# Splitting the tables' operands once on 128 rows, and a first DFT step on four row tiles of 32

## The chip, the cores and the metric

The kernel runs on one core of a Trainium2 chip. Its time is the device time of one execution in microseconds (us). A timed run and the profiled execution are different executions; the profile's times are counted from the start of the profiled span.

The core's engines work side by side, each through its own instructions in order: PE multiplies matrices (PEld is its loading of weights), DVE, ACT and POOL work on vectors, SP issues most DMA transfers here. ACT and POOL can issue transfers too. Results of PE land in PSUM and are copied ("evacuated") to SBUF by ACT or DVE.

## What is computed

Two independent parts, whose outputs stand side by side:

```python
def _A_ref(x, wqkv, wo):            # x: (1, 2048, 576), 32 heads of 18, window W = 256
    qkv = (x @ wqkv).reshape(B, S, 3, H, Dh).transpose(2, 0, 3, 1, 4)
    scores = einsum("bhqd,bhkd->bhqk", q, k) * Dh ** -0.5
    mask = (q_pos - k_pos >= 0) & (q_pos - k_pos < W)
    p = softmax(where(mask, scores, -1e9))
    return (p @ v).transpose(0, 2, 1, 3).reshape(B, S, D) @ wo

def _B_ref(u, A_re, A_im, B_re, B_im, C_re, C_im, log_dt, Dskip):   # D = 576, N = 128, L = 2048
    dt = exp(log_dt)[:, None]
    P = exp((dt * A)[:, :, None] * arange(L))            # complex
    K = einsum("dn,dnl,dn->dl", C, P, dt * B).real       # 2048 taps for each channel
    y = irfft(rfft(pad(u)) * rfft(pad(K)))[:L]           # causal convolution over L
    return y + u * Dskip

out = concatenate([_A_ref(...), _B_ref(...)], axis=-1)
```

Part A is attention over a sliding window; part B makes a kernel of 2048 taps for each of 576 channels from exponentials and convolves u with it.

## The kernel before

The program has four stages.

**Opening** (`front`, lines 208 to 300, an order written out by hand). It loads the projection's weights `wqkv` in four pieces into the tile `K`, x (two pieces `raw` for the first 512 columns, and the rest as four pieces `flat`, which share two buffers), and the parameters of part B. `amax` finds the largest absolute value of each piece on DVE; POOL reduces over the partitions (`pow2_max`), and from that a power of two scales weights and x. `split_w` and `split_x` split each into an f16 value and an f16 remainder: the first on ACT, the remainder on DVE.

In the same order the operands of the tables are made: `al` from A_re times dt, `ps` from A_im times dt over 2 pi. Both are bf16 tiles of 96 rows with three levels of the same 32 channels: rows 64 to 95 hold the rounded value, rows 0 to 31 the rounded remainder of it, rows 32 to 63 the remainder of that, so that one matmul over 96 rows adds up the levels. The host gives the inputs three times (96 x 18 x 128), and the subtractions run on 64 and then 32 of these rows: `al`'s on DVE (lines 255, 263, 271), `ps`'s on POOL (lines 265, 267, 279), the copies on ACT (256, 264, 266, 272, 278, 280).

**Joint stage** (lines 1006 and 1007). Three generators are merged in proportion to their lengths: `proj` (14 matmuls for each group of 128 output rows and 512 columns of x; line 171; results to DRAM as `qd` and `vd`), `tables` (36 chunks of 16 channels: exponentials on ACT, sines and cosines on ACT, products on POOL at line 411 and on DVE at 431 to 434, and then the taps, 64 small f32 matmuls at line 449), and `s1_u`, the first DFT step of u. The tables' first pieces, `exps_ab` and `exps_q` (12 matmuls and 12 exponentials), are part of this stage. PE's instructions keep the order that the program's scheduler gave them; the opening and the start of the attention stage keep the order of the code.

**First DFT step** (`s1`, lines 486 to 495). A step takes 4 of 64 values of l, 576 columns of f32. The 128 rows are four groups of 32 (four groups of channels, each with 32 points). Weight `w1` is 128 x 128 with the 32 x 32 cosine matrix four times on the diagonal, and another one with the sines. A step is two parts (cosine, sine) of two matmuls of 288 columns each, every one into its own PSUM buffer of the pool `pps` (three buffers, shared with the projection). `evac` copies each to SBUF, three of four on ACT and one on DVE, and one transfer a part, 288 KB, takes the 128 rows to DRAM: `gx` for u (16 steps in the joint stage), `gk` for the taps (16 steps after it, of which ten are merged with `gmax(0)`, the row maxima of the first attention unit: line 668 on PE, 675 on DVE).

**Attention and convolution** (line 1031). `load` (line 516) fetches for each of 16 pairs of frequencies the pieces `tx` of `gx` and `tk` of `gk`, 576 KB each in one transfer; the other DFT steps are interleaved with the attention.

Transfers issued by SP and ACT share a ring of semaphores: a transfer waits until the one that used the same semaphore before it has landed.

## Time and profile before

| | |
|---|---|
| median of 3 runs | 1023.63 us (1023.08 to 1027.1) |
| profiled execution | 1029.98 us |
| its span | 1028.3 us |
| mean granted PE clock | 0.968 |
| busy: PE, PE weight loads, DVE, ACT, POOL | 838.4, 449.0, 697.9, 568.5, 601.5 us |
| moved by DMA | 150.56 MB, 146 GB/s over the span |

The span lies 1.7 us inside the profiled execution's own time, which is 6.3 us above the median.

A row of a timeline has start, length, engine, line, operation, output <- input, shape, and in brackets the idle time of the engine before it with what ended it. "x8" counts instructions: an f32 matmul appears as two. Lengths of matmuls include the time until the result is out, so that neighbours overlap and a busy PE can stand for less work than its busy time. A row of a group has the summed busy time, the mean of one in ns, and the idle time of the engine ahead of them. A row of the stretches has the busy time and the count of instructions of each engine, the granted PE clock, the share of time in which the DMA engines were busy, and the rate.

### The profile page before, as it was taken

Reading aid. Unit: us, or ns where it says so; the run is one execution under the profiler, and the core shown is the slowest. Engines: PE = TensorE matmul, PEld = TensorE weight load, DVE = VectorE, ACT = ScalarE, POOL = GpSimd, SP = SyncE. Lnnn points to the kernel's source line nnn. Section 1 sums busy time; section 2 is a strip of 40 time slices with the busy share of each in tenths; the row PEclk is TensorE's granted clock in tenths of the full one; section 3 lists DMA queues with packets and bytes.
Section 4 is the critical chain, followed back from the end, with each engine's and each line's share of the span. In section 5 each row is a group of like instructions: output and inputs, shape, how many; then the busy total and the mean of one; then the engine's idle time right before and its main releaser. Section 6 shows DMA issues by size and latency. Waiting matters only on the chain.

```text
span 1028.3 us, 26833 instructions
## 1 busy us (share of the span) xinstructions
PE 838.4 (82%) x10364; PEld 449.0 (44%) x10364; DVE 697.9 (68%) x1799; ACT 568.5 (55%) x893; POOL 601.5 (58%) x717
## 2 busy tenths in 40 slices
PE   0079979999996989687888887778888999988687
PEld 0034644565564557454333333333333444444245
DVE  5957594676667565545677788778777766777454
ACT  0546675776765765234565555555655655644470
POOL 0424784786666666300567666767686766766670
PEclk9999999999998999989999899999999999999899
DMA  9744544545452433757444556446444464678863
GB/s 308 230 108 108 122 117 96 120 99 132 104 123 61 106 83 75 201 173 215 114 124 124 175 153 198 129 114 186 134 140 145 131 187 113 161 196 224 224 179 126
DMA packets 144711, 150.56 MB, mean 146 GB/s; under 512 B 36408, under 2 KB 121144, under 8 KB 143624
## 3 DMA queue, kind: packets, MB, share of 16 engines
q1 hardware_dynamic: 137896, 133.51, 47.1%
q0 software_dynamic: 6128, 14.60, 5.1%
q8 instruction: 81, 1.33, 0.5%
q10 hardware_dynamic: 560, 0.74, 0.2%
q14 instruction: 46, 0.38, 0.1%
HBM read 87.42 MB, written 61.01 MB: 144 GB/s over the span
## 4 chain that ended last, share of the span: by engine, by line
PE 25%; DVE 12%; issue 6%; DMA 6%; ACT 3%; POOL 2%; SPq 1%; DVEq 0%; POOLq 0%; ACTq 0%
PE r L668 5%; PE po L732 5%; PE r L938 4%; PE r L532 3%; PE r L540 3%; PE ST L709 3%; DVE jk L675 2%; PE pp L493 2%; DVE qb L659 2%; ACT P L711 1%; DVE osb L791 1%; DMA tx<-gx 1%; DMA raw<-in_wo_dram 1%; POOL P L720 1%; DVE t L562 1%
## 5 line engine op out<-in xcount | busy, mean ns | idle before, releaser
L675 DVE CUSTOM_DVE_ANT_0 jk<-r,bias 128x288 f32<-128x288 f32 (+7 forms) x512 | 199.9, 433 | 91.1 <-PE r L668 89.0
L720 POOL TENSOR_SCALAR_AFFINE_SELECT P<-P 128x512 f32<-128x512 f32 x240 | 167.2, 726 | 154.4 <-ACT P L711 151.9
L711 ACT ACTIVATE P<-ST,esc 128x1024 f32<-128x1024 f32 (+1 forms) x192 | 202.4, 1059 | 91.3 <-PE ST L709 90.7
L411 POOL TENSOR_TENSOR m<-A,tr 128x1024 f32<-128x1024 f32 x72 | 143.9, 2022 | 76.6 <-PE kp L449 76.6
L668 PE MATMUL r<-K,qb 128*64 128x288 f16 (+7 forms) x1024 | 129.2, 297 | 43.8 <-DVE qb L659 11.9
L668 PEld LDWEIGHTS <-qb 128*64 128x64 f16 x1024 | 59.8, 109 | 126.8 <-issue 68.3
L732 PE MATMUL po<-P,V 128*32 128x256 f32 (+2 forms) x1408 | 101.8, 404 | 15.7 <-ACT osb L740 6.0
L569 POOL TENSOR_TENSOR Y<-t,t 64x288 f32<-64x288 f32 x64 | 54.4, 850 | 74.7 <-DVE t L564 72.8
L493 PE MATMUL pp<-ut,w 128*128 128x288 f32 x128 | 41.5, 446 | 65.8 <-DMA ut<-in_u_dram 52.4
L449 PE MATMUL kp<-Q,m 128*32 128x64 f32 x4608 | 82.8, 225 | 9.2 <-DVE Q L432 5.2
L449 PEld LDWEIGHTS kp<-Q,m 128*32 128x32 f32 x4608 | 71.5, 113 | 34.9 <-issue 23.8
L709 PE MATMUL ST<-Q,K 64*128 64x384 f16 (+2 forms) x704 | 73.3, 282 | 0.0
L732 PEld LDWEIGHTS po<-P,V 128*32 128x32 f32 x1408 | 36.6, 111 | 50.7 <-issue 32.4
L493 PEld LDWEIGHTS pp<-ut,w 128*128 128x128 f32 x128 | 23.3, 199 | 79.8 <-issue 53.4
L136 ACT ACTIVATE g<-pp 128x288 f32<-128x288 f32 x96 | 37.4, 413 | 37.3 <-PE pp L493 27.8
L389 POOL TENSOR_TENSOR tr<-tr,mab 128x768 f32<-128x768 f32 x18 | 33.2, 1845 | 39.8 <-ACT tr L358 39.8
L570 POOL TENSOR_TENSOR Y<-t,t 64x288 f32<-64x288 f32 x64 | 53.6, 838 | 3.7
L352 DVE TENSOR_TENSOR k<-x,k 128x512 f32<-128x512 f32 (+1 forms) x54 | 33.9, 639 | 28.9 <-ACT k L351 28.7
L353 DVE TENSOR_SCALAR ab<-k 128x512 int32<-128x512 int32 (+1 forms) x54 | 53.0, 993 | 0.4
L171 PE MATMUL pp<-xh,wh 128*128 128x512 f16 x180 | 48.9, 392 | 4.1 <-DVE qst L318 2.7
L171 PEld LDWEIGHTS <-wh 128*128 128x128 f16 x324 | 31.6, 99 | 45.2 <-issue 11.7
L318 DVE SCALAR_TENSOR_TENSOR qst<-pp,qst 128x512 f16<-128x512 f32 x36 | 24.6, 685 | 36.0 <-ACT qst L317 21.3
(172 smaller groups left out, 1757.5 us busy)
## 6 DMA issues: line engine op xcount, KB each, us to landing
gx<-g SPq DMA_DIRECT2D x32, 288.0 KB
qd<-qst SPq DMA_DIRECT2D x72, 128.0 KB
gk<-g SPq DMA_DIRECT2D x32, 288.0 KB
tx<-gx SPq DMA_DIRECT2D x16, 576.0 KB
tk<-gk SPq DMA_DIRECT2D x16, 576.0 KB
h<-ho SPq DMA_DIRECT2D x16, 576.0 KB
Q<-qd SPq DMA_DIRECT2D x32, 216.0 KB
raw<-in_x_dram SPq DMA_DIRECT2D x8, 640.0 KB
```

The source lines that it names most:

```text
L171: self.nc.tensor.matmul(ps, u, v, start=(i == 0), stop=(i == len(ops) - 1))
L411: self.nc.gpsimd.tensor_tensor(m, A[:, ch, a0:a0 + 8].unsqueeze(3).to_broadcast(sh), tr[:, ch, part, 0:8].unsqueeze(2).to_broadcast(sh), o ...
L449: nc.tensor.matmul(kp[32 * st:32 * st + 32, c % 2 * JJ2 + j, :], m[:, ch, a0:a0 + 32], Q[:, ch, term % 2, :], start=(term == 0), stop=(ter ...
L493: nc.tensor.matmul(ps, self.w1[:, part, :], src[:, o:o + k], start=True, stop=True)
L569: nc.gpsimd.tensor_tensor(Y[par][0:64], t1[sl, 0], t2[sl, 0], op=OP.subtract)
L570: nc.gpsimd.tensor_tensor(Y[par][64:128], t1[sl, 1], t2[sl, 1], op=OP.add)
L668: nc.tensor.matmul(ps[64 * b:64 * b + 64, :n], self.qb[:, b, t, :], d["K"][:, b, k0:k0 + n], start=True, stop=True, skip_group_check=True)
L675: nc.vector.tensor_tensor_reduce(out=jk[:, :n], in0=ps[:, :n], in1=self.bias[:, 288 - n:], scale=1.0, scalar=-3e38, op0=OP.add, op1=OP.max ...
L709: nc.tensor.matmul(ps[:, u, o:o + n], d["K"][h, jp, k0:k0 + 128], d["Q"][h, jp, q0:q0 + n], start=True, stop=True, skip_group_check=True)
L711: nc.scalar.activation(pt[:, 2 * jp:2 * jp + 2, lo:hi], ps[:, :, lo:hi], AF.Exp, scale=self.esc)
L720: nc.gpsimd.affine_select(v, v, pattern=[[0, 4], [sg, 128]], compare_op=OP.is_ge, fill=0.0, base=-1 if far else 0, channel_multiplier=-sg)
L732: nc.tensor.matmul(self.po[32 * j:32 * j + 32, t0 * 128:t1 * 128], V[:, kb * 76 + 19 * j:kb * 76 + 19 * j + 32], pt[:, j, o:o + (t1 - t0) ...
```

## The change

**Operands of the tables.** The host now lays A_re, A_im and log_dt out on 128 rows (`by_group`): four blocks of 32 rows with five groups of channels each (the last block has three), 128 x 5 x 128, once and not three times. On these tiles `level(i)` multiplies by dt (i = 0) or subtracts the last level, on DVE for both operands, and rounds to bf16 on ACT into one of six small tiles `part`. Four transfers for each level and operand spread the blocks to rows 32 i to 32 i + 31 of `al` (issued by ACT) and `ps` (issued by POOL): 24 transfers of 32 rows, SBUF to SBUF. POOL's tensor operations in the opening are gone. The loads of A_re and A_im are issued by ACT ahead of the constants.

**Order of the opening.** The tables' first twelve pieces (`exps_ab(0)`, `exps_ab(1)`, `exps_q(0)`) are called from `front`, between the splits of the weights. The four pieces of `flat` have a buffer each. The remainders of the weights' last two pieces (`split_w(2, 1)` and `(3, 1)`) are called from `proj`. The first merge ahead of the long one takes six parts of the projection and four of the tables, and none of `s1_u`; before, it took 7, 16 and 1. The long merge has 50, 308 and 16 parts instead of 49, 308 and 15.

**First DFT step.** `w1` is 128 x 64: in each block of 32 rows the cosines and then the sines. A half step is four matmuls of 32 rows (one block each) and 64 columns, at four row positions and, in turns, two column positions; two of them fill the two halves of one PSUM buffer. A step has eight matmuls instead of four, four evacuations as before, and four transfers of 64 rows (144 KB) instead of two of 128. For the taps the second half's two buffers come from a new PSUM pool `s1p`. `gx` and `gk` have a new layout (64, 4, 64, 144), and `load` fetches `tx` and `tk` in two transfers of 64 rows each.

```diff
-    w1 = np.zeros((128, 2, 128))
-    for s in range(4):
-        w1[s * 32:s * 32 + 32, 0, s * 32:s * 32 + 32] = np.cos(ph)
-        w1[s * 32:s * 32 + 32, 1, s * 32:s * 32 + 32] = np.sin(ph)
+    w1 = np.tile(np.concatenate([np.cos(ph), np.sin(ph)], axis=1), (4, 1))
...
+def by_group(v):
+
+    w = np.zeros((4, 5, GC, v.shape[1]), np.float32)
+    w.reshape(20, GC, -1)[:NQ] = v.reshape(NQ, GC, -1)
+    return np.ascontiguousarray(w.transpose(0, 2, 1, 3).reshape(128, -1))
...
         for c in range(4):
-            flat.append(tp.tile([128, 2304], F32, name="flat%d" % (c % 2))[:, :cols[c + 1] - cols[c]])
+            flat.append(tp.tile([128, cols[c + 1] - cols[c]], F32, name="flat%d" % c))
...
+        parts = [[tp.tile([128, 5, 128], BF, name="part%d%d" % (e, i)) for i in range(3)] for e in range(2)]
+        ops = [(nA["A_re"], dtn, al, nc.scalar), (nA["A_im"], dtp, ps, nc.gpsimd)]
+
+        def level(i):
+
+            for e, (z, d, T, eng) in enumerate(ops):
+                if i == 0:
+                    tt(z, z, wide(d), op=OP.mult)
+                else:
+                    tt(z, z, parts[e][i - 1], op=OP.subtract)
+                act(parts[e][i], z, AF.Copy)
+            for e, (z, d, T, eng) in enumerate(ops):
+                for r in range(4):
+                    n = min(5, NQ - 5 * r)
+                    eng.dma_start(T[32 * i:32 * i + 32, 5 * r:5 * r + n], parts[e][i][32 * r:32 * r + 32, :n])
+
+        self.mab, self.mg = {}, {}
+        exps = chain(self.exps_ab(0), self.exps_ab(1), self.exps_q(0))
         for c in range(4):
             self.amax(amx[:, c:c + 1], wf[:, c])
+            if c < 3:
+                level(c)
...
+        next(exps), next(exps)
         self.split_w(0, 0)
...
-    def s1(self, src, g, l0, nl, pool):
+    def s1(self, src, g, l0, nl, pool, psum):
+
         nc, n = self.nc, nl * 144
-        for part in range(2):
-            st = self.p[pool].tile([128, n], F32, name="g1")
-            k = n // 2 if n <= 576 else n // 3
-            for o in range(0, n, k):
-                ps = self.p["pps"].tile([128, 512], F32, name="pp")[:, :k]
-                nc.tensor.matmul(ps, self.w1[:, part, :], src[:, o:o + k], start=True, stop=True)
-                self.evac(st[:, o:o + k], ps)
-            nc.sync.dma_start(g[part, l0:l0 + nl].rearrange("l p j -> p l j"), st.rearrange("p (l j) -> p l j", j=144))
+        st = [self.p[pool].tile([128, n], F32, name="g%d" % e) for e in range(2)]
+        k = n // 2
+        for i in range(2):
+            ps = [self.p[psum[i]].tile([128, 512], F32, name="pp")[:, :k] for _ in range(2)]
+            for q in range(4):
+                r, h = slice(32 * q, 32 * q + 32), 64 * (q % 2)
+                nc.tensor.matmul(ps[q // 2][h:h + 64], self.w1[r], src[r, i * k:i * k + k], start=True, stop=True,
+                                 skip_group_check=True)
+            for e in range(2):
+                self.evac(st[e][:, i * k:i * k + k], ps[e])
+        for q in range(4):
+            h = 64 * (q % 2)
+            nc.sync.dma_start(g[l0:l0 + nl, q].rearrange("l p j -> p l j"),
+                              st[q // 2][h:h + 64].rearrange("p (l j) -> p l j", j=144))
...
-                nc.sync.dma_start(t[nm], g.rearrange("a l (s f) j -> (a l) s f j", s=4)[:, :, 2 * fp:2 * fp + 2, :])
+                for e in range(2):
+                    f0 = 32 * e + 2 * fp
+                    nc.sync.dma_start(t[nm][64 * e:64 * e + 64], g[:, :, f0:f0 + 2])
...
-                merge((part(proj, 7), 7), (part(tables, 16), 16), (part(s1u, 1), 1))
-                merge((proj, 49), (tables, 308), (s1u, 15))
-            self.pool(ek, "s1k", 4, side="right")
+                merge((part(proj, 6), 6), (part(tables, 4), 4))
+                merge((proj, 50), (tables, 308), (s1u, 16))
+            self.pool(ek, "s1k", 2, side="right")
+            self.pool(ek, "s1p", 2, PSUM, side="right")
```

The numbers of lines in what follows are those of the kernel before.

More of the change, by code (lines that the diff above doesn't have):

```diff
@@ L2 @@
 from contextlib import ExitStack
+from itertools import chain
 import ml_dtypes
@@ L1000, in build @@
                 proj, tables, s1u = self.proj(), self.tables(), self.s1_u()
+                for n in ("mab", "mg"):
+                    self.pool(e1, n, 4)
                 with ExitStack() as e2, self.tc.manual_schedule():
```

69 lines of the change are left out of this document (28 added, 41 removed).

## The prediction

> **What bounds the kernel now.** I read the profile by stages: the busy time per stretch first, then the timeline of the opening, the groups of the joint stage, and the chain of waits through the first DFT step of the kernel taps. The stretches (length; busy time of PE, PE weight loads, DVE, ACT, POOL, each with its count; granted PE clock; DMA share; GB/s):
>
> ```profile
> 25.00:52.00 27.00, 0.00 (x0) 0.00 (x0) 25.83 (x12) 14.04 (x7) 10.47 (x2) 1.00 0.72 228
> 52.00:60.00 8.00, 4.03 (x9) 2.35 (x10) 4.76 (x9) 5.58 (x6) 0.38 (x1) 1.00 0.20 44
> 60.00:92.00 32.00, 29.04 (x115) 12.12 (x114) 17.51 (x23) 17.34 (x27) 7.25 (x2) 0.95 0.46 112
> 92.00:420.00 328.00, 294.62 (x5731) 187.12 (x5730) 215.05 (x312) 213.39 (x383) 231.37 (x187) 0.98 0.44 104
> 420.00:437.00 17.00, 12.21 (x38) 7.45 (x38) 8.53 (x11) 4.83 (x12) 0.00 (x0) 0.90 0.90 257
> 437.00:467.00 30.00, 26.70 (x131) 16.91 (x132) 14.44 (x70) 10.99 (x27) 0.00 (x0) 0.89 0.58 169
> 475.00:1028.00 553.00, 465.33 (x4320) 218.62 (x4316) 395.30 (x1344) 294.89 (x420) 349.54 (x518) 0.97 0.55 158
> ```
>
> Four stages follow each other. In the opening (to 60 us) PE does almost nothing and DVE is full. From 60 to 420 PE is full and every other engine has room: this is the joint stage of projection, tables and u's first DFT step. From 420 to 475 runs the kernel's first DFT step, held by DMA until 437 and then by a loop through PE and DVE. The attention stage behind it is not rewritten, so I let it move as a whole.
>
> The opening in the timeline (start, length, engine and line):
>
> ```profile
> 18.30 2.40 DVE L161 TENSOR_REDUCE amx<-K 128x1 f32<-128x2160 f32 x1 [1.45 <-DMA K<-in_wqkv_dram]
> 22.12 2.55 DVE L255 TENSOR_TENSOR nA_re<-nA_re,dtn 96x2304 f32<-96x2304 f32 x1 [1.23 <-DMA nA_re<-in_n_A_re_dram]
> 25.23 2.87 DVE L161 TENSOR_REDUCE amx<-raw 128x1 f32<-128x1280 f32 x2
> 28.85 2.47 DVE L192 SCALAR_TENSOR_TENSOR wl<-K,wr,wh 128x2160 f16<-128x2160 f32 x1 [0.75 <-ACT wh L190]
> 31.23 6.39 DVE L263 TENSOR_TENSOR res<-nA_re,al 64x2304 f32<-64x2304 f32 x1
> 37.55 5.00 DVE L161 TENSOR_REDUCE amx<-flat 128x1 f32<-128x2304 f32 x2
> 40.11 0.35 SPq L231 DMA_DIRECT2D flat<-in_xf_dram  x1
> 42.57 6.31 DVE L271 TENSOR_TENSOR res<-res,al 32x2304 f32<-32x2304 f32 x1
> 48.91 2.61 DVE L161 TENSOR_REDUCE amx<-flat 128x1 f32<-128x1152 f32 x2
> 51.56 0.16 DVE L145 TENSOR_REDUCE xm<-amx 128x1 f32<-128x6 f32 x1
> 54.38 2.61 ACT L201 ACTIVATE xh<-raw,xr 128x1280 f16<-128x1280 f32 x2 [5.75 <-DVE xr L157]
> 60.29 0.15 PEld L171 LDWEIGHTS <-wh 128*128 128x128 f16 x1
> ```
>
> The projection cannot start before x's maximum is known (51.56) and x is split (54.38 on). DVE reaches that maximum late because two subtractions on whole tables, 6.39 and 6.31 us, stand ahead of it, and because the third piece of `flat` is issued only at 40.11, when DVE has read the first two.
>
> ```profile
> 65.71 1.24 PE L171 MATMUL pp<-xh,wh 128*128 128x512 f16 x5
> 68.73 1.24 PE L171 MATMUL pp<-xh,wh 128*128 128x512 f16 x5
> 70.89 1.03 PE L171 MATMUL pp<-xl,wh 128*128 128x512 f16 x4
> 74.57 2.02 PE L171 MATMUL pp<-xh,wh 128*128 128x512 f16 x5 [2.66 <-DVE qst L318]
> 90.39 1.82 POOL L389 TENSOR_TENSOR tr<-tr,mab 128x768 f32<-128x768 f32 x1 [24.12 <-ACT tr L358]
> 92.27 2.39 PE L493 MATMUL pp<-ut,w 128*128 128x288 f32 x8
> ```
>
> A row group of the projection is 14 matmuls. The first takes 5.4 us (60.29 to 65.71), the second 3.02 (to 68.73), and after the third (ended 71.92) PE waits until 74.57. The tables' twelve exponentials are interleaved only then, so POOL gets its first table at 90.39. The second, long merge begins on PE at 92.27 and lasts to the first matmul of the kernel's DFT near 419.8: 327.5 us.
>
> **The opening after the change.** On DVE two multiplications and four subtractions of 128x640 take the place of 96x2304. By the 2.55 us of the multiplication one costs 2.55 x 640/2304 = 0.71; by the 6.39 us of the subtraction 1.78. I take 0.71 for all, since the two long subtractions ran beside POOL's own tensor work, which is gone. Six are 4.3 us and lie between the four maxima of the weights, where DVE waits for loads (1.45 us ahead of the last). So the weight maxima still end near 20.7. At the dear price 8.5 us lie there, some 4 more than the gaps hide.
>
> The 24 spreading transfers are issued half by ACT and half by POOL. POOL's last four stand ahead of the reduction over partitions; a POOL issue costs 0.61 us by this group, 2.4 us for four:
>
> ```profile
> L798 POOL DMA_DIRECT2D od<-oh x52 | 31.6, 610 | 0.0
> L358 ACT ACTIVATE mg<-x 128x512 f32<-128x512 f32 x64 | 35.9, 599 | 4.9 <-PE x L341 4.3
> ```
>
> That puts the weights' scale near 25.3, where it was (DVE went on at 25.23). Then DVE runs raw maxima 2.87, flat maxima 5.00 + 2.61, and three `wl` of 2.47 (one is pulled ahead of x's maximum in the new order): 25.3 + 2.87 + 7.61 + 7.41 = 43.2 instead of 51.56. With four buffers no `flat` waits for DVE. ACT's twelve exponentials, at most 12 x 0.60 = 7.2 us, fit in, since ACT is busy 14.04 of 27.00 there. From the maximum to the split takes 54.38 - 51.56 = 2.82, the split 2.61: the projection starts near 50 with some reserve for late operands (60.29 before; bounds 47 and 56, the latter if ACT's issues are held behind loads).
>
> From there to the long merge the old order had six row groups, the exponentials and two idle stretches, 32.0 us. The new one has five row groups and no exponentials: one at 5.4 (slow at first, as it will be again) and four at 3.02, 17.5, plus about 1.5 for stalls on evacuation: 69 instead of 92.3, bounds 65 and 80 (the earliest and the latest start above, without stalls and with the old idle time beside it). **Opening: -23**, of which +3.0 comes back, since one row group more stands inside the long merge.
>
> **First DFT step of u.** Before: four matmuls of 128x128 a step; after: eight of 32 rows and 64 columns, each half the output. What concurrency looks like here:
>
> ```profile
> 545.41 1.19 PE L532 MATMUL r<-tk,w 128*64 128x288 f32 x8
> 547.38 0.39 PE L709 MATMUL ST<-Q,K 64*128 64x384 f16 x4
> 547.95 1.21 PE L540 MATMUL r<-Y,i 128*128 128x288 f32 x4 [0.18 <-DVE t L565]
> ```
>
> Eight instructions on two column tiles take 1.19, four on the whole array 1.21: two column tiles run side by side in f32. Row tiles are shown only in pairs of 64 rows and in f16 (four in 0.39 us). Row tiles of 32 in f32 are shown nowhere. The step's PE time was 2.14 (eight instructions, 0.267 each); all four side by side it is 1.07, pairs only 2.14, none 4.28. I take 1.25.
>
> But a step costs the joint stage more than its matmuls:
>
> ```profile
> L493 PE MATMUL pp<-ut,w 128*128 128x288 f32 x112 | 34.8, 430 | 13.4 <-ACT g L136 8.8 <-DVE qst L318 2.6 <-ACT vst L329 1.9
> 218.25 1.46 PE L493 MATMUL pp<-ut,w 128*128 128x288 f32 x4
> 220.39 1.54 PE L493 MATMUL pp<-ut,w 128*128 128x288 f32 x4 [0.67 <-ACT vst L329]
> ```
>
> Fourteen steps are 34.8 busy and 13.4 waiting for PSUM buffers, 3.44 each (the one at 218.25 took 3.6). Now a half step takes two of the three buffers at once, and the second half waits for the projection's tile and for the first evacuation. I take 2.8: fifteen steps at 3.44 were 51.6, sixteen (one more lies in the merge) at 2.8 are 44.8. **u: -7**; bounds +3 (still 3.44) and -20 (2.0, matmuls plus the evacuations' 0.4).
>
> The Trainium skill, TensorEngine Tiling (Array Packing), section PSUM Bottleneck, says that tiling speeds up the matmuls but not the emptying of PSUM. By its rule all four evacuations remain and the gain is smaller than the 0.9 us of PE time; the idle column above agrees.
>
> **First DFT step of the kernel.** One round of the loop with the row maxima:
>
> ```profile
> 454.24 2.14 PE pp L493 x8
> 456.38 0.39 PE r L668 x4
> 456.79 0.45 DVE jk L675
> 457.30 0.31 PE r L668 x2
> ```
>
> ```profile
> 454.96 1.43 ACT L136 ACTIVATE g<-pp 128x288 f32<-128x288 f32 x3 [1.94 <-PE pp L493]
> 437.01 0.71 ACT L136 ACTIVATE g<-pp 128x288 f32<-128x288 f32 x2 [5.04 <-DMA gk<-g]
> 480.00:484.00 4.00, 3.44 (x30) 1.43 (x28) 3.51 (x20) 1.80 (x2) 0.64 (x1) 0.87 0.99 319
> ```
>
> A round is 3.37 us (454.24 to 457.61), of which 2.14 is the step. At 1.25 it is 2.5; ACT's 1.43 and two extra PSUM buffers fit. Seven such rounds give 6.2, the two longer rounds before 444 some 2, the burst at the end 1. The first 17 us stay, because there the stores set the pace (5.04 us for a landing). A step stores 0.59 MB, in 2.5 us 236 GB/s, against 319 at a full DMA share; four issues like that at 40.11 (0.35) take 1.4. I take 2 off: **kernel: -7**, bounds 0 and -9.
>
> In the convolution each fetch becomes two, 32 issues more on SP, of 0.35 us like that at 40.11, 11 us spread over more than 350; no engine's wait is added, so 0 to +3 for a later landing, taken as 0.
>
> **Sum:** -23 + 3 - 7 - 7 = -34. The profiled execution took 1029.98 (span 1028.3), so it would be 996; the median of the runs is 1023.63, 6.3 lower, so 990.
>
> **The rivals.** (1) *Row tiles gain nothing.* Only two of the four tiles run at a time, because two share the columns, or because the first and second write one PSUM tile and the third and fourth the other: u stays 3.44 a step (+3), the kernel's round 3.37. -23 + 3 + 3 = -17: 1007. For it: no f32 row tile in the trace; against: the pairs at 547.38, though these write two PSUM banks. The Trainium skill, TensorEngine Tiling (Array Packing), Gotcha 1: PSUM Pressure, says that different row tiles cannot use one PSUM bank at the same time; by it this rival would hold, and no row here shows two row tiles in one bank.
>
> (2) *Operands late.* ACT's issues wait for loads ahead of them and hold the copies, exponentials and `wh` behind them on ACT; PE waits for all three levels. The opening gives 5 instead of 23: 1008. For it: the DMA share is still 0.72 after 25 us, when these transfers run; against: each is only 41 KB (32 rows of 640 bf16).
>
> (3) *Stores in halves are slow.* Every transfer of the DFT now spans 64 partitions. If one ran at half of 319 GB/s, 9.4 MB of stores take 59 us plus the loads among them, +8 instead of -7, and the attention's first fetch +7: -23 + 3 - 7 + 8 + 7 = -12: 1012. Against it: two are in flight together. The Trainium skill, DMA: Bandwidth & Descriptors, Rules for kernel authors, says that transfers to disjoint partition halves serialize and one of 128 partitions should be used; it speaks for this rival, and no row here compares the two.
>
> (4) *Slower: no overlap at all.* If the four f32 row tiles follow one another, a step is 4.28: u 16 x 5.58 - 51.6 = +38, the kernel's later eleven steps 11 x 2.14 = +24 and the first five +4. -23 + 3 + 38 + 28 = +46: 1070. With 27 steps that count (sixteen and eleven), -20 is used up at 2.14 + (20 - 3)/27 = 2.8 us a step; from there it decides. Against it: 545.41.
>
> **How the numbers follow.** Forecast 0.57; (1) 0.13, (2) 0.11, (3) 0.09, (4) 0.08; 0.02 for no change. The forecast's own range is 978 to 1000. Including (1), (2) and most of (3) the range is 975 to 1013; what is left out is (4) and the tails. Within 0.5% means 5 us, about what can be told from no change. Faster gets 0.85, same 0.05, slower 0.10.
>
> **What would show it.** The first `wh` load near 50 and POOL's first table near 63; the u group's busy plus idle near 2.8 us a step; rounds of 2.5 us; the kernel's DFT beginning near 392 and ending near 440; the attention stage still 553. Wrong if an eight-matmul burst takes over 2 us, if the first `wh` comes after 56, or if the attention stage grows by over 5.

## The result, and the profile after the change

| | kernel before | changed kernel |
|---|---|---|
| median on the same chip | 1024.83 us | 1029.84 us |
| ratio of the times | | 1.0063, 95% interval 1.0046 to 1.0080 |
| profiled execution, its span | 1029.98, 1028.3 us | 1032.46, 1030.7 us |
| mean granted PE clock | 0.968 | 0.948 |
| to the projection's first matmul | 60.8 us | 60.2 us |
| joint stage, to the first matmul on the taps | 359.0 us | 361.7 us |
| first DFT step of the taps, to the first score matmul | 53.1 us | 52.5 us |
| attention and convolution, to the end | 555.4 us | 556.3 us |

The change makes the kernel slower by 0.6%, about 5 us, where 34 us faster was forecast; the time lies above the range. No stage is shorter by more than 1 us. The stages are those of one profiled execution each. The one of the kernel before lies 5.2 us above its median and that of the changed kernel 2.6, so the stages show only 2.4 of the 5 us. The stretches of the changed kernel, at the same times as in the prediction (length; busy time of PE, weight loads, DVE, ACT, POOL; granted clock; DMA share; GB/s):

```profile
25.00:52.00 27.00, 7.11 (x15) 1.77 (x16) 13.94 (x13) 13.17 (x17) 2.34 (x5) 1.00 0.75 244
52.00:60.00 8.00, 0.00 (x0) 0.00 (x0) 5.98 (x9) 2.42 (x2) 0.35 (x1) 1.00 0.00 0
60.00:92.00 32.00, 29.55 (x189) 12.44 (x191) 24.69 (x36) 16.08 (x28) 15.36 (x13) 1.00 0.53 125
92.00:420.00 328.00, 294.80 (x5772) 173.78 (x5761) 205.44 (x300) 205.57 (x372) 215.07 (x171) 0.94 0.46 103
437.00:467.00 30.00, 20.70 (x204) 9.53 (x204) 15.25 (x73) 10.35 (x28) 0.00 (x0) 0.75 0.84 196
```

DVE, full from 25 to 52 before (25.83 us busy), is now busy for 13.94 of 27 us: its two long subtractions are gone, and yet the projection starts no earlier. From 92 to 420 PE is busy as long as before (294.80 against 294.62 us), but the granted clock has fallen from 0.98 to 0.94. From 437 to 467 PE has 6 us less to do, and the DMA engines are busy for 0.84 of the time instead of 0.58.

The changed kernel's opening, in its own line numbers (150 the maxima's last reduction, 151 POOL's reduction over partitions, 158 its first use, 176 the projection, 206 the split of x, 269 the spreading transfers):

```profile
25.10 0.16 DVE L150 TENSOR_REDUCE wm<-amx 128x1 f32<-128x4 f32 x1
26.70 1.96 POOL L269 DMA_DIRECT2D ps<-part  x4 [2.67 <-ACT part L265]
37.76 0.38 POOL L151 PARTITION_ALL_REDUCE wg<-wm  x1 [9.11 <-issue]
38.17 0.15 DVE L158 TENSOR_SCALAR wg<-wg 128x1 f32<-128x1 f32 x1 [12.92 <-POOL wg L151]
56.18 0.15 DVE L150 TENSOR_REDUCE xm<-amx 128x1 f32<-128x6 f32 x1
60.25 1.86 PE L176 MATMUL pp<-xh,wh 128*128 128x512 f16 x4 [9.22 <-ACT xh L206]
```

The weights' maximum is there at 25.10, when the forecast had its scale (25.3). But POOL first issues its last four spreads (1.96 us), and then does nothing that the profile names for 9.11 us ("issue": it waits for nothing that the profile shows) before it reduces. DVE stands idle for 12.92 us. Everything behind it takes what the prediction gave it: from the scale to x's maximum it is 56.18 - 38.17 = 18.0 us, forecast 43.2 - 25.3 = 17.9. The joint stage and the first DFT steps, by groups (busy, mean, idle time ahead and its causes), and two rounds of the taps' loop:

```profile
L509 PE MATMUL pp<-ut,w 32*64 32x288 f32 x256 | 30.7, 440 | 9.5 <-DVE qst L333 4.7 <-ACT g L141 4.1
L141 ACT ACTIVATE g<-pp 128x288 f32<-128x288 f32 x48 | 17.8, 409 | 34.7 <-DMA gk<-g 24.7 <-PE pp L509 9.9
452.69 1.20 PE L509 MATMUL pp<-K,w 32*64 32x288 f32 x16
455.16 1.20 PE L509 MATMUL pp<-K,w 32*64 32x288 f32 x16
460.35 1.20 PE L509 MATMUL pp<-K,w 32*64 32x288 f32 x16
463.56 1.20 PE L509 MATMUL pp<-K,w 32*64 32x288 f32 x16
```

A burst of eight matmuls takes 1.20 us (1.25 forecast, 2.14 before): four row tiles in f32 do run side by side. A step of u costs PE (30.7 + 9.5) / 16 = 2.5 us with its waits, less than the 2.8 of the forecast. In the loop of the taps the first round is 2.47 us, as forecast, the last one shown 3.21, and the evacuations wait 24.7 us for the stores of `g` (7.2 before).

So three questions are open: what holds the reduction, why less PE work in u does not shorten the joint stage, and what the stores cost.

### The profile page after: what moved, and what is told of

It is laid out like the page before. It is cut to its first block, busy times and chain, and to the rows that moved or that the text cites. A ratio compares the mean times of both kernels' runs of the same rounds, so it can differ in the third digit from the quotient of the medians.

```text
span 1030.7 us, 27519 instructions
## 1 busy us (share of the span) xinstructions
PE 833.3 (81%) x10620; PEld 423.5 (41%) x10620; DVE 688.7 (67%) x1802; ACT 556.8 (54%) x893; POOL 589.1 (57%) x726
## 4 chain that ended last, share of the span: by engine, by line
PE 43%; DVE 19%; issue 12%; DMA 11%; ACT 8%; SPq 4%; POOL 2%; DVEq 0%; ACTq 0%; POOLq 0%
PE pp L176 11%; PE r L691 5%; PE po L755 5%; PE r L961 4%; PE kp L466 4%; PE r L555 3%; PE ST L732 3%; PE r L563 3%; PE x L358 2%; DVE jk L698 2%; PE pp L509 2%; DMA gk<-g 2%; SPq L130 2%; ACT P L734 1%; DVE qb L682 1%
## 5 line engine op out<-in xcount | busy, mean ns | idle before, releaser
L691 PE MATMUL r<-K,qb 128*64 128x288 f16 (+7 forms) x1024 | 131.7, 304 | 45.3 <-DVE t L586 11.5
L466 PE MATMUL kp<-Q,m 128*32 128x64 f32 x4608 | 80.2, 222 | 8.0 <-issue 3.6
L176 PE MATMUL pp<-xh,wh 128*128 128x512 f16 x180 | 51.7, 408 | 16.5 <-ACT xh L206 10.7
L755 PEld LDWEIGHTS po<-P,V 128*32 128x32 f32 x1408 | 36.2, 110 | 50.1 <-issue 33.2
L141 ACT ACTIVATE g<-pp 128x288 f32<-128x288 f32 x96 | 35.7, 411 | 37.4 <-DMA gk<-g 24.7
L333 DVE SCALAR_TENSOR_TENSOR qst<-pp,qst 128x512 f16<-128x512 f32 x36 | 24.7, 686 | 45.8 <-ACT qst L332 42.0
L555 PE MATMUL r<-tx,w 128*64 128x288 f32 x256 | 42.4, 440 | 11.5 <-ACT X L582 5.4
L176 PE MATMUL pp<-xh,wl 128*128 128x512 f16 x180 | 51.5, 413 | 0.0
L370 DVE TENSOR_SCALAR ab<-k 128x512 int32<-128x512 int32 (+1 forms) x54 | 47.5, 892 | 0.3
```

Of the source, the lines that this page charges most:

```text
L176: self.nc.tensor.matmul(ps, u, v, start=(i == 0), stop=(i == len(ops) - 1))
L466: nc.tensor.matmul(kp[32 * st:32 * st + 32, c % 2 * JJ2 + j, :], m[:, ch, a0:a0 + 32], Q[:, ch, term % 2, :], start=(term == 0), stop=(ter ...
L555: nc.tensor.matmul(ps[64 * par:64 * par + 64], w2[:, par, 64 * part:64 * part + 64], t[:, 2 * hs:2 * hs + 2, par, :], start=True, stop=True)
L691: nc.tensor.matmul(ps[64 * b:64 * b + 64, :n], self.qb[:, b, t, :], d["K"][:, b, k0:k0 + n], start=True, stop=True, skip_group_check=True)
L755: nc.tensor.matmul(self.po[32 * j:32 * j + 32, t0 * 128:t1 * 128], V[:, kb * 76 + 19 * j:kb * 76 + 19 * j + 32], pt[:, j, o:o + (t1 - t0) ...
```

## Experiments

All times are against the kernel before on the same chip. A stage's length is that of one profiled execution; the attention stage, where the matmuls are the same, varies between 549.7 and 557.3 us from kernel to kernel, so differences of a few us within one stage need the ratio beside them. Where a ratio is turned into us, 0.01 is 10.2 us. The joint stage varies too where its program hardly differs: in the four kernels that have the new front and the u step as changed it lasts 357.1 to 361.7 us.

### The opening: ps spread by SP

```diff
-        ops = [(nA["A_re"], dtn, al, nc.scalar), (nA["A_im"], dtp, ps, nc.gpsimd)]
+        ops = [(nA["A_re"], dtn, al, nc.scalar), (nA["A_im"], dtp, ps, nc.sync)]
```

> The changed kernel with the spreads of ps issued by SP instead of POOL. Theory A (POOL's last spreads stood ahead of the partition reduction, and the change of POOL's configuration between the two, 26.70 to 37.76, was what cost the opening its gain): the reduction runs within 2 us of its operand, at 25 to 27 us instead of 37.76, and the projection's first matmul starts at 47 to 51 instead of 60.25. The rival (the configuration takes its time whenever the reduction is called, whatever stands ahead of it): the reduction stays near 35 to 38 and the first matmul near 60. For the time: if the joint stage hands an earlier start on to its end, the span falls by 9 to 13 us, to 1018 to 1022; if the joint stage is paced by something that does not start with the projection, less than 4 us of it arrive.

Ratio 0.9958 (0.9938 to 0.9978): 10.7 us faster than the changed kernel. Its timeline:

```profile
25.49 0.16 DVE L150 TENSOR_REDUCE wm<-amx 128x1 f32<-128x4 f32 x1
25.79 0.38 POOL L151 PARTITION_ALL_REDUCE wg<-wm  x1 [22.56 <-DVE wm L150]
46.73 0.15 DVE L150 TENSOR_REDUCE xm<-amx 128x1 f32<-128x6 f32 x1
50.80 1.44 PE L176 MATMUL pp<-xh,wh 128*128 128x512 f16 x3 [5.22 <-ACT xh L206]
65.45 1.81 POOL L406 TENSOR_TENSOR tr<-tr,mab 128x768 f32<-128x768 f32 x1 [18.11 <-ACT tr L375]
71.00 0.70 PE L509 MATMUL pp<-ut,w 32*64 32x288 f32 x4
```

With no transfer ahead of it POOL reduces 0.14 us after its operand is ready, and the projection starts at 50.8 us instead of 60.2. Theory A holds as to the place: the spreads' issues ahead of the reduction cost the time. What POOL does in those 9.11 us no row shows. The forecast's dates are met too, for POOL's first table (63, measured 65.45) and for the long merge (69; the first u step, which stands at its start, comes at 71.0). x's maximum comes later than forecast (46.73 against 43.2), and the matmul follows it sooner (4.1 us against 5.4). Even so the joint stage lasts 357.1 us, 2 us less than before. Nearly the whole gain is the 10 us of the earlier start.

### One half of the change alone

The first kernel keeps the new front and takes the old DFT steps with their constants, layout and pools; the second is the old front with the new DFT steps.

```diff
-            ps = [self.p[psum[i]].tile([128, 512], F32, name="pp")[:, :k] for _ in range(2)]
...
+                nc.tensor.matmul(ps, self.w1[:, part, :], src[:, o:o + k], start=True, stop=True)
```

> The changed kernel with the first DFT steps of u and K as they were before (128-row operands with zeros, four matmuls and two stores of 128 rows a step): the tables' operands and the order of the front alone. If the loss sits in the new first DFT steps (clock in the joint stage, stores of 64 rows after it): faster than before by 2 to 8 us, with the kernel's first DFT again under 55 us and its matmuls waiting on stores 7 us in all instead of 25. If the loss sits in the front and in the new place of the u steps: as slow as the changed kernel, 1028 to 1034.

> The kernel before with the new first DFT steps alone (row tiles, four stores of 64 rows a step, fetches in halves), the front as before. By the sum of the prediction (u steps -7, rounds of K -7): 14 us faster than before, 1009 to 1014. By the reading of the two traces, in which the stores of 64 rows moved 233 GB/s for a full share against 291 and the u steps' shorter matmuls turned into waits: within 4 us of before, and the stretch after K is complete no shorter than the 53 us of before.

Front alone: 0.9993 (0.9970 to 1.0015), no difference from before and 7 us faster than the changed kernel. That is short of the 2 to 8 us under the kernel before that one expectation had, and far from the 1028 to 1034 of the other. DFT steps alone: 1.0146 (1.0123 to 1.0169), 15 us slower, which none of the expectations had. The new front takes over half of that loss away, so the two parts are not independent. The joint stages (from the first matmul of the projection to the first on the taps) of before, front alone, DFT alone and both, and of the changed kernel with the spreads from SP:

```profile
60.80:419.80 359.00, 322.66 (x5842) 198.71 (x5840) 231.62 (x334) 230.55 (x409) 238.45 (x188) 0.98 0.44 104
60.30:417.00 356.70, 324.99 (x5835) 199.34 (x5834) 231.08 (x337) 222.60 (x399) 232.13 (x187) 0.97 0.45 107
56.10:432.40 376.30, 332.41 (x5966) 190.73 (x5965) 234.40 (x336) 232.68 (x411) 237.40 (x188) 0.94 0.44 100
60.20:421.90 361.70, 324.85 (x5963) 186.54 (x5962) 231.50 (x336) 222.49 (x399) 232.12 (x187) 0.95 0.47 105
50.80:407.90 357.10, 318.68 (x5967) 185.22 (x5966) 230.47 (x336) 222.40 (x399) 231.93 (x187) 0.97 0.47 106
```

Such a row gives a sum. The length less PE's busy time is idle time. The length times one minus the granted clock, added up over stretches of about 4 us, is what the clock took at most. The rest is PE's work at full clock:

| joint stage, us | length | idle | clock | work |
|---|---|---|---|---|
| before | 359.0 | 36.3 | 8.6 | 314.1 |
| new front, old DFT steps | 356.7 | 31.7 | 12.1 | 312.9 |
| old front, new DFT steps | 376.3 | 43.9 | 23.9 | 308.5 |
| changed kernel | 361.7 | 36.9 | 19.1 | 305.8 |
| changed, spreads from SP | 357.1 | 38.4 | 12.0 | 306.7 |

The new u steps take 6 to 7 us of work out of the stage, about as forecast (-7). Idle time and clock give back about that or more. The size of the clock's part is uncertain: with the same u steps it is 19.1 us in the changed kernel and 12.0 with the spreads from SP. The new front takes 1.2 us of work out, although it also brings in one u step (about 2.5 us) that lay ahead of the projection before. The forecast had the long merge begin 13 us earlier beyond the projection's own start.

### Stores of 128 rows

```diff
-        for q in range(4):
-            h = 64 * (q % 2)
-            nc.sync.dma_start(g[l0:l0 + nl, q].rearrange("l p j -> p l j"),
-                              st[q // 2][h:h + 64].rearrange("p (l j) -> p l j", j=144))
+        for e in range(2):
+            nc.sync.dma_start(g[l0:l0 + nl, 2 * e:2 * e + 2].rearrange("l q p j -> (q p) l j"),
+                              st[e].rearrange("p (l j) -> p l j", j=144))
```

> The changed kernel with each pair of its 64-row stores put together into one of 128 rows (two of 288 KB a step, as before in size; the layout in DRAM stays). Theory B (64-row stores cost more DMA time, and the kernel's first DFT was bound by them): the wait of the evacuations for the stores' buffers falls from 24.7 us to under 8, rounds take 2.5 us, and the kernel's first DFT is 5 to 12 us shorter. The rival (the DMA time comes from the place in DRAM that a store writes to, not from its rows): the rounds stay at 2.5 to 3.2 us and the DMA rate near 196 GB/s at a share of 0.84.

1.0000 (0.9982 to 1.0018): 6 us faster than the changed kernel, with the projection's start almost as late as there (58.6 us). The taps' first DFT in before, the changed kernel and this one, and the evacuations' waits in this one:

```profile
419.00:475.00 56.00, 45.58 (x200) 29.04 (x201) 27.56 (x92) 22.21 (x51) 0.80 (x3) 0.91 0.69 200
```

```profile
421.00:475.00 54.00, 36.92 (x322) 16.53 (x322) 27.13 (x92) 18.70 (x49) 0.70 (x3) 0.72 0.83 200
```

```profile
418.00:467.00 49.00, 34.40 (x324) 15.10 (x324) 27.05 (x92) 17.84 (x50) 0.27 (x1) 0.81 0.78 226
L141 ACT ACTIVATE g<-pp 128x288 f32<-128x288 f32 x48 | 17.3, 410 | 30.5 <-DMA gk<-g 18.5 <-PE pp L509 12.0
```

Rate by share (all transfers of the stage, most of them stores) is 200 / 0.69 = 290 GB/s before, 200 / 0.83 = 241 with 64-row stores and 226 / 0.78 = 290 with 128-row stores, which write to the same places in DRAM as the 64-row ones. So theory B is right about the cause. Its size for the wait was wrong (18.5 us, under 8 expected): the first third of the stage stays bound by stores, and the stage itself is shorter by 4.7 us (47.8 against 52.5), just under the 5 to 12 expected.

### Both repairs, the old u step, and u twice

The next kernels have both repairs. In the second, u's step is the old one (128-row operands with zeros, two stores, fetched whole) beside row tiles for the taps. In the third, u's rounds of four matmuls are issued twice.

```diff
-            self.s1(ut.rearrange("p l j -> p (l j)"), self.gx, l0, 4, "s1s", ("pps", "pps"))
+            self.s1_old(ut.rearrange("p l j -> p (l j)"), self.gx, l0, 4, "s1s")
```

```diff
-            for q in range(4):
+            for q in (0, 1, 2, 3) * (2 if pool == "s1s" else 1):
```

> The changed kernel with both repairs: spreads of ps from SP, and stores of 128 rows. If the opening's 10 us (first projection matmul at 50.8 instead of 60.2) and the 5 us of the kernel's first DFT (47.8 us instead of 52.5) lie one behind the other on the path: 14 to 17 us faster than the changed kernel, a ratio of 0.988 to 0.992 to the kernel before. If one hides the other: no better than 0.995.

> As the kernel with both repairs, but the first DFT step of u in its old form (128-row operands with zeros, pieces fetched whole); K's first DFT stays in row tiles. By the prediction's sum (a u step saves PE time, and PE paces the joint stage): 7 us slower than with both repairs, joint stage 364 against 357. By theory C (the PE time that the new u step saves comes back as idle time and as granted clock, since PE only reaches its next wait sooner): within 3 us of it either way, joint stage 354 to 360, with 6 to 9 us more of PE work net of the clock and as much less idle time and clock loss.

> As the kernel with both repairs, with each round of four matmuls of the u steps issued twice (16 steps, about 1.25 us more PE work each by the burst of 1.20 us for eight matmuls: 19 to 20 us in all; the result does not change). If PE's work paces the joint stage: 17 to 20 us slower, joint stage 374 to 377. Theory C: the stage takes less than half of it, 0 to 9 us, and PE's idle time and clock loss shrink by the rest.

Both repairs: 0.9900 (0.9878 to 0.9923). The two add up. Old u step: 0.9845 (0.9822 to 0.9868), 5.6 us faster still, where the prediction's sum said 7 slower and theory C no more than 3 either way. u twice: 1.0030 (1.0013 to 1.0047), 13 us slower than with both repairs, between the two expectations. The joint stages of the three:

```profile
50.20:411.00 360.80, 324.64 (x5967) 186.72 (x5966) 230.06 (x335) 222.34 (x399) 231.85 (x187) 0.95 0.44 105
51.20:406.50 355.30, 324.65 (x5836) 199.31 (x5835) 229.98 (x335) 222.41 (x399) 231.91 (x187) 0.97 0.45 107
49.70:425.60 375.90, 341.24 (x6219) 199.28 (x6218) 225.00 (x335) 223.84 (x399) 230.22 (x187) 0.95 0.42 101
```

| joint stage, us | length | idle | clock | work |
|---|---|---|---|---|
| both repairs | 360.8 | 36.2 | 18.9 | 305.7 |
| with the old u step | 355.3 | 30.7 | 12.0 | 312.7 |
| with u's matmuls twice | 375.9 | 34.6 | 17.2 | 324.1 |

The old step has 7.0 us more work and 12.4 us less idle time and clock loss, about 7 of them clock, the part that varies most. But 18 us of added work lengthen the stage by 15, so PE's work does count: theory C, that changes of PE's work come out as idle time and clock, is too simple. Something about the undivided new step costs extra.

### u in halves, in quarters, and the old step divided

The step hands over to the other streams after each half; its parts in the merge become 32.

```diff
             for e in range(2):
                 self.evac(st[e][:, i * k:i * k + k], ps[e])
+            if i == 0:
+                yield
...
-                merge((proj, 50), (tables, 308), (s1u, 16))
+                merge((proj, 50), (tables, 308), (s1u, 32))
```

> As the kernel with both repairs, with each u step placed in two halves (32 parts instead of 16 in the interleaving, two psum buffers asked for at a time, then other work). If the waits of the second half for the shared psum buffers (4.8 + 4.4 us on PE with the spreads from SP) hold the joint stage up: these waits fall under 3 us and the stage is 4 to 8 us shorter, 349 to 353 us. If the stage is paced elsewhere (the tables' ACT and DVE chain): within 3 us of 357.

> As the kernel with both repairs and the old u step, with that old step placed in two halves too (one part of the output, two psum buffers, then other work; 32 parts). Theory D (row tiles are worth the 7 us of PE work they save, but only where the step is placed in halves): dividing does little for the old step, ratio to the kernel before 0.982 to 0.987, PE work net of the clock 312 to 314, so 3 to 6 us slower than row tiles in halves (0.981). The rival (dividing helps any form, and row tiles bring the joint stage nothing): 0.974 to 0.981.

> As the kernel with both repairs and u steps in halves, with each u step in four parts instead of two (one psum buffer and two row tiles at a time, 64 parts). If what counts is how many psum buffers a part asks for: as fast as halves or up to 4 us faster, 0.977 to 0.981. If the concurrency of four row tiles counts: the u matmuls cost some 0.5 us more a step, 8 us in all, 0.984 to 0.990.

> As the kernel with both repairs and the old u step in halves, with that step in four parts of one matmul and one psum buffer each (64 parts). With row tiles the quarters cut PE's idle time in the joint stage from 35 to 20 us, but took 18 us more PE work. If the number of psum buffers that a piece takes at once sets the waits: idle time falls from 30 to about 20 here too, PE work stays at 309 to 314, joint stage 334 to 340, ratio 0.966 to 0.971. If the idle time fell there only because PE worked longer (other engines set the pace): joint stage 344 to 349, ratio 0.974 to 0.978.

| u step, both repairs | ratio (95% interval) | joint stage, us | idle | clock | work |
|---|---|---|---|---|---|
| row tiles, whole | 0.9900 (0.9878 to 0.9923) | 360.8 | 36.2 | 18.9 | 305.7 |
| row tiles, halves | 0.9808 (0.9784 to 0.9832) | 347.1 | 35.1 | 8.6 | 303.4 |
| row tiles, quarters | 0.9831 (0.9806 to 0.9857) | 349.7 | 19.5 | 8.5 | 321.7 |
| old, whole | 0.9845 (0.9822 to 0.9868) | 355.3 | 30.7 | 12.0 | 312.7 |
| old, halves | 0.9752 (0.9731 to 0.9773) | 345.7 | 29.6 | 6.8 | 309.3 |
| old, quarters | 0.9712 (0.9688 to 0.9737) | 342.6 | 27.7 | 4.5 | 310.4 |

The joint stages of row tiles and of the old step in halves, and the matmuls of u there: row tiles whole (both repairs), row tiles in halves, old step in halves:

```profile
50.80:397.90 347.10, 312.00 (x5967) 180.81 (x5966) 231.78 (x336) 221.29 (x399) 231.07 (x187) 0.98 0.46 110
50.50:396.20 345.70, 316.07 (x5835) 196.98 (x5834) 231.45 (x335) 221.50 (x399) 231.25 (x187) 0.98 0.47 110
```

```profile
L509 PE MATMUL pp<-ut,w 32*64 32x288 f32 x256 | 30.8, 442 | 10.0 <-ACT g L141 4.7 <-DVE qst L333 4.7
```

```profile
L509 PE MATMUL pp<-ut,w 32*64 32x288 f32 x256 | 27.5, 431 | 1.1 <-DVE qst L333 0.6 <-ACT vst L346 0.4 <-ACT g L141 0.2
```

```profile
L528 PE MATMUL pp<-ut,w1u 128*128 128x288 f32 x128 | 37.9, 413 | 1.4 <-DVE qst L337 0.8 <-ACT vst L350 0.3 <-ACT g L145 0.3
```

Dividing is worth 9 us with either form. Half a step asks for two buffers, and the next matmuls in PE's order no longer stand behind its second half: u's waits fall from 10.0 us to 1.1. But PE's idle time as a whole hardly falls (36.2 to 35.1 us): PE waits elsewhere instead. Of the 13.7 us by which the stage of the row tiles shrinks, 10.3 are clock (3.4, if the undivided step's clock loss is taken from the kernel with the spreads from SP, 12.0 us); of the 9.6 us with the old form 5.2 are. That the gain comes from breaking up the waits on PE, behind which the clock drops, agrees with these numbers and is argued, not shown. Theory D falls. u's matmuls with their waits cost 28.6 us as row tiles and 39.3 in the old form, and yet the old form is 5.7 us faster as a whole, while its joint stage is 1.4 us shorter. The rest lies in the taps' stage (1.2 us) and in the attention stage (2.8), which is within what that stage varies. Quarters help the old step a little more (0.9712, between the two expectations). With row tiles a quarter issues only two tiles at a time, u's matmuls take 46.9 us instead of 27.5, and the kernel is slower than with halves (0.9831, between the two expectations).

The same halves in the changed kernel, with nothing else, and in the old front with 128-row stores (the second diff is the change of the merge there):

```diff
-                merge((part(proj, 7), 7), (part(tables, 16), 16), (part(s1u, 1), 1))
-                merge((proj, 49), (tables, 308), (s1u, 15))
+                merge((part(proj, 7), 7), (part(tables, 16), 16), (part(s1u, 2), 2))
+                merge((proj, 49), (tables, 308), (s1u, 30))
```

> The changed kernel with nothing but its u steps placed in halves. If the division's gain (9 us with both repairs) is independent of the opening and of the stores: 0.996 to 0.999, joint stage 348 to 353, kernel's first DFT still 51 to 53. If it needs the earlier start: over 1.002.

> The kernel before, its front untouched, with the first DFT steps in row tiles as mended (u steps in halves, stores of 128 rows). If the 15 us that the row tiles cost with the old front came from the undivided u step and the 64-row stores: all of it is gone and the DFT steps show their own gain, 0.986 to 0.993, joint stage 347 to 352, kernel's first DFT 47 to 49. If the old front itself clashes with the shorter u steps: 0.996 or more, joint stage over 357.

Halves alone: 1.0005 (0.9983 to 1.0026), 6 us less than the changed kernel, somewhat under the expectation. Old front: 0.9912 (0.9886 to 0.9938), as expected, so the 15 us that the DFT steps alone cost came from the undivided u step and the stores. Its profiled joint stage, 359.1 us, was longer than expected; that execution took 1022.4 us, 7.5 above its kernel's median of 1014.9.

### The taps' matmuls twice, and the fetches

With row tiles in halves and both repairs, the rounds of the taps' DFT are issued twice (the edit shown for u, with the pool `s1k`).

> As the kernel with both repairs and u steps in halves, with each round of four matmuls of the kernel's first DFT issued twice (same result; about 1.2 us of PE work more in each of 16 steps). The clock in the first 17 us of that stage was 0.90 with the old matmuls and 0.70 to 0.76 with row tiles, at nearly the same busy time. If the granted clock follows PE's busy time: it rises to 0.85 or more there, and the stage grows by under 8 us. If it follows the form of the matmuls (32 rows, 64 columns): it stays at 0.70 to 0.78, and the stage grows by 10 us or more.

0.9831 (0.9806 to 0.9856), 2 us slower. The loop's part of the stage, without and with the doubling:

```profile
414.90:439.50 24.60, 20.21 (x194) 9.14 (x192) 14.00 (x69) 9.23 (x26) 0.00 (x0) 0.77 0.68 200
```

```profile
414.70:442.70 28.00, 24.23 (x342) 12.97 (x334) 14.09 (x70) 10.16 (x27) 0.00 (x0) 0.98 0.64 191
```

In the loop the clock rises from 0.77 to 0.98 with the same form of matmul, so the form alone does not hold it down there. That it follows PE's busy time is not shown: PE is busy for 0.82 of the loop without the doubling and 0.87 with it, and the kernel before, busy for 0.89, had 0.89. In the first 17 us, where stores set the pace, it stays at 0.73 although PE is busy for 14.18 us; there neither theory is decided. The stage grows by 3.4 us for sixteen steps of about 1.2 us more matmuls each, so most of the added work found room in time that PE had to spare.

The last two concern the attention's fetches. One takes both operands of the row-tile kernel whole, the other halves the first operand's fetch in the kernel with the old u step in halves.

```diff
-                    nc.sync.dma_start(t[nm][64 * e:64 * e + 64], g[:, :, f0:f0 + 2])
+                nc.sync.dma_start(t[nm], g.rearrange("l s (a f) j -> a l s f j", a=2)[:, :, :, 2 * fp:2 * fp + 2])
```

```diff
-            nc.sync.dma_start(t["tx"], gx[:, :, 2 * fp:2 * fp + 2, :])
+            for e in range(2):
+                nc.sync.dma_start(t["tx"][64 * e:64 * e + 64], gx[64 * e:64 * e + 64, :, 2 * fp:2 * fp + 2, :])
```

> As the kernel with both repairs and u's row tiles in halves (0.9808), with each piece of the attention's first and second operand fetched by one transfer over 128 rows instead of two over 64. The prediction took the halved fetches as 0, with a bound of 3 us: then the ratio stays at 0.979 to 0.982. If they are what separates this kernel from the old u step in halves (0.9752): 0.975 to 0.977, attention stage 2 to 4 us shorter.

> As the kernel with both repairs and the old u step in halves (0.9752), with the attention's first operand fetched in two transfers of 64 rows instead of one of 128 (16 transfers more on SP). If the halved fetches are what row tiles cost: 0.978 to 0.981, attention stage 554 to 556. If they cost nothing, as the prediction took it: 0.974 to 0.977, and the difference lies in the joint stage, where the saved PE work comes back as idle time.

The first is 21% slower (1.2083, 1.2053 to 1.2114). It was the wrong test: the order of the new layout makes an access pattern whose slowest dimension has two entries, and these transfers land late. Its attention stage and two steps of the chain of waits (start, length):

```profile
447.70:1233.30 785.60, 498.85 (x4322) 231.22 (x4321) 397.17 (x1346) 297.14 (x421) 349.22 (x518) 0.82 0.38 112
485.13 28.54 DMA tk<-gk
596.12 28.17 DMA tk<-gk
```

The second gives 0.9776 (0.9733 to 0.9819), with the attention stage at 552.1 us against 551.9. The interval holds both expectations, so what the halved fetches cost stays open within about 4 us. Nothing is seen of it in the stage itself.

## Why the prediction was wrong, by its steps

**Opening, -23 + 3: the step that failed first.** The prediction said "a POOL issue costs 0.61 us by this group, 2.4 us for four" and put the scale at 25.3. The issues took 1.96 us. Put at nothing, without a reason, was the time between POOL's last issue and the reduction, 9.11 us. Its like is visible in the trace of before, in rows that the prediction did not use, where the reduction and a tensor operation follow other work:

```profile
53.20 0.38 POOL L146 PARTITION_ALL_REDUCE xg<-xm  x1 [6.73 <-issue]
60.63 5.64 POOL L279 TENSOR_TENSOR res<-res,ps 32x2304 f32<-32x2304 f32 x1 [7.05 <-issue]
```

There it cost little: the reduction's operand came (51.72) after most of the 6.73 us had passed, so that it ran 1.5 us late. In the changed kernel the operand was there first. The spreads from SP show that this alone cost 10 us. The rest of the order was priced well in sum (50.8 against near 50).

The other 13 us were for the most part never there to win. The prediction's own row for 60 to 92 us shows PE busy for 29.04 of 32.00 at a clock of 0.95, so no more than 4.6 us of that stretch were idle or lost to the clock. Taking the exponentials and a u step out of it and starting the long merge earlier (by 10 us in the changed kernel, by 21 with the spreads from SP) moves work. The work of the stage fell by 1.2 us with the new front alone, and its length by 2.3, no more than the stage's own scatter. The step took the start of a merge for progress of the stage.

**u, -7.** The PE time was right: 1.20 us for a burst, 2.5 a step with its waits, 6 to 7 us of work saved. The sum then took PE's time for the stage's. The stage gained nothing, since idle time and clock came back: 45 us before, 56 in the changed kernel (50 with the spreads from SP). The clock had no term in the sum. Most of the loss goes with the step's being undivided (9 us with both repairs). Yet even divided the row tiles bring the joint stage no gain over the old form. Why the saved work comes back as idle time is not settled; that PE merely reaches its next wait sooner agrees with the table and is no more than argued, and doubling u's work shows that the opposite direction does cost.

**Taps, -7.** The mechanism and the round (2.5 us) were right, the place was taken by the stores. The prediction allowed 2 us for them, with the 319 GB/s of another stretch for a full share; with stores of 64 rows the stage reached 241. In place the step gave -0.6; with 128-row stores -5.3.

**Fetches, 0.** The attention stage moved as a whole (556.3 against 555.4), within what it varies.

**The account.** Against before the changed kernel has +5. The POOL reduction takes 10.7 of it, the stores 6, the undivided u step 6 to 9; with all three mended it is at 0.9808, 20 us faster than before. These are differences between kernels, and they need not add up exactly. Of the 34 us the rest are mainly the 10 of the front that PE's row did not hold, and u's 7, of which little is left.

**The rivals.** (1) and (4) fell with the burst of 1.20 us. There the trace disagrees, as far as the rule's wording goes, with the Trainium skill, TensorEngine Tiling (Array Packing), Gotcha 1: PSUM Pressure: the first two row tiles of each round write one PSUM tile at the same time. They write different halves of its rows; row tiles that write the same rows were not tried. (2) came nearest to the opening's loss, by another cause. (3) was the right mechanism at a smaller price: with stores of 64 rows the stage lost a sixth of its rate (241 against 290 GB/s), where it supposed a half, and 6 us with it. The advice of the Trainium skill, DMA: Bandwidth & Descriptors, Rules for kernel authors, which spoke for it, to use one transfer of 128 partitions, held: the merged stores brought 290 GB/s for a full share. That the halves serialize no run here shows. That three losses could come together was in no case, and so the range was too low.

The fastest kernel here has the old u step in quarters, row tiles for the taps, 128-row stores and the new front with `ps` spread by SP: 0.9712 (0.9688 to 0.9737), 992.07 us.

## What to carry over

Before counting an earlier start as a gain, read from the stretch's own row how much idle time and lost clock it holds; what is moved out of it comes back later. A short piece of work that asks for several shared buffers at once blocks everything behind it on its engine, so try dividing it before making it faster. And price an instruction on POOL together with what stood before it there: four issues of 0.5 us each put a reduction off by 11.

## What the runs showed of the hardware

- Between other work on POOL and a reduction over partitions lay 6.7 to 9.1 us that the profile puts down to nothing (9.11 ahead of 37.76 in the changed kernel, 6.73 ahead of 53.20 before), and 7.05 us between a reduction and other work. Where POOL had stood idle for 22.56 us, the reduction began 0.14 us after its operand.
- Row tiles of 32 rows and 64 columns in f32 run four at a time, also two in one PSUM tile: eight matmuls in 1.20 us. Two at a time (quarters) the sixteen steps of u take 46.9 us instead of 27.5.
- The granted clock halved after a gap on PE of 1.89 us. In the kernel with both repairs:

```profile
196.00:197.00 1.00, 1.00 (x13) 0.45 (x12) 1.00 (x3) 0.06 (x1) 0.92 (x3) 1.00 0.01 1
198.00:199.00 1.00, 0.00 (x0) 0.00 (x0) 0.98 (x2) 1.00 (x2) 0.91 (x3) 1.00 0.31 74
200.00:201.00 1.00, 0.94 (x13) 0.31 (x5) 1.00 (x3) 0.86 (x3) 1.00 (x1) 0.50 0.08 16
```

PE is idle from about 197.2 to 199.0 and then works at half clock for some 6 us. The Trainium skill, TensorE: Matmul & The Clock Gate, HAM oscillation, gives idle gaps of over about 3.4 us as the danger; here 1.9 were enough, right behind u's matmuls. With u in halves a gap of 1.71 us at the same place left the clock at 1.00:

```profile
193.00:194.00 1.00, 0.00 (x1) 0.00 (x0) 0.33 (x2) 0.94 (x2) 0.92 (x3) 1.00 1.00 235
195.00:196.00 1.00, 1.00 (x61) 0.86 (x50) 0.93 (x2) 1.00 (x4) 1.00 (x1) 1.00 0.40 74
```

What decides between the two was not tried.

- A transfer whose slowest dimension has two entries stood in the chain of waits for 28 us (576 KB, about 20 GB/s over that time). It agrees with the Trainium skill, DMA: Bandwidth & Descriptors, Rules for kernel authors, by which such a dimension confines a transfer to at most as many DMA engines as it has entries. On how many engines it ran no row here shows.
